# Block-sorted attention and feed-forward: the key products of batches 1 to 3, each split into two matmuls of 64 rows and 64 moving columns

## The chip, the core and the metric

One core of one Trainium2 chip runs one program. The metric is device time in microseconds (us) of one execution: lower is better. The median of three runs of the kernel before is 221.51 us (221.34 to 221.83). One further execution was recorded by the hardware profiler; every number about single instructions comes from that one.

The engines of the core have short names in the profile: PE is the matmul engine, PEld its loads of stationary weights (which run beside PE), DVE the vector engine, ACT the scalar engine, POOL the GpSimd engine, SP the engine whose queue issues DMAs here.

## The reference, cut to what matters

```python
# q, k, v: (4 batches, 8 heads, 768 positions, 64); sort_net: (4, 8, 8, 8)
P = sort_net, normalised five times by exp, rows and columns
k_sorted = einsum('bhij,bhjcd->bhicd', P, k_b)   # 8 blocks of 96 positions, mixed per head
v_sorted = einsum('bhij,bhjcd->bhicd', P, v_b)
scores = softmax(scale * q_b @ k_sorted_b^T)      # block by block, 96 x 96
attn_out = scores @ v_sorted_b                    # x: (3072, 512)
h = maximum(x @ w_in, 0)                          # 512 -> 2048
out = (s * h * h + b) @ w_out                     # 2048 -> 512
```

What matters here is `k_sorted`: for each batch, head and position in a block, the eight blocks' keys are mixed by the head's own 8 x 8 matrix `P`.

## The kernel before, in words

**Layout of the keys.** `RAW["k", b]` holds batch `b`'s keys as 128 partitions by 48 positions by 64 dimensions. A partition is one (head, block, half of the block): 8 heads x 8 blocks x 2 halves, so that partitions 0 to 63 hold heads 0 to 3 and partitions 64 to 127 heads 4 to 7. Mixing the blocks is a matmul that contracts over the partitions. Its moving operand is `PD[b]` (`build_pd`, L273), 128 partitions by `(e, z, g)`: `e` is the parity of the head, `z` the half of the block, `g` the pair of heads times the output block (`NG` = 32). A head's rows meet zeros in every column of another head: of the 128 x 128 numbers, the quarter for rows 0 to 63 and `g` of 16 to 31 is zero, and likewise rows 64 to 127 with `g` of 0 to 15.

**The product that the change touches.** `k_pairs(b, c0, engs)` (L310) makes 16 of the 48 positions. It takes positions two at a time as one stationary operand of 128 columns (2 positions x 64 dimensions), so eight matmuls of 128 rows, 128 stationary and 128 moving columns at L314 fill one PSUM tile `tpp`: two banks, from the pool `psa`, which has three such tiles. Four casts then copy the tile into `KS[b % 2]`, the sorted keys: 64 partitions by 512 numbers each, two on DVE (L205) and two on ACT (L203), through `evac`. `k_pairs` runs three times in a row (`KP(n, 0)`, `KP(n, 1)`, `KP(n, 2)`) for each of batches 1, 2 and 3; batch 0 uses `k_piece` and `k_banks`.

**The order of the work.** Nothing is scheduled automatically: the program's text is the order on each engine, and semaphores wait where data or buffers demand it. The feed-forward works on halves of a batch (`t` = 0 to 7, 384 rows each). `ffn1(t)` (L505) makes eight pieces `hps` at L501 and squares them on ACT (L513) and DVE (L514); `ffn2(t)` (L519) sums 16 matmuls of 512 columns for each of three row blocks at L525 and stores them (`store`, L548). The attention of batch `n` is put between these matmuls by hand: `ffn1` and `ffn2` take `slots`, lists of pieces that are issued after a given step. In `ffn2`, slot 0 comes behind the first four matmuls.

- For batch 1 the three key products stand in slot 3 of `ffn2(0)` and three value products (`v_piece`, L340, tiles `tv`, also from `psa`) in slot 9. The fourth value product and the scores come in `ffn2(1)`.
- For batches 2 and 3 the three key products stand in slot 0 of `ffn2(2b)`. The values take another way: `v_tiles` (L367) in `ffn1(2b)`, then `v_back` (L375), which sends them through DRAM on SP's queue (`vd` at L379, `vs` at L383).
- `s_piece` (L391) makes scores at L405 from `KS` and the transposed queries `qt`: matmuls of 64 rows and 96 moving columns, alternating between rows 0 to 63 and rows 64 to 127, which write different banks of the tile `sc`. `s_banks` (L423) is the same for batch 0. The first two score pieces of batch `n` stand in slot 0 of the `ffn2` that follows the one with the key products. `p_piece` (L433, matmuls at L450) follows in later slots.
- `qt` of batches 1 to 3 comes from `q_dma` (L480), two transposing DMAs on SP's queue (L484) behind `vd` and `vs`. They read `qtok`, which POOL's queue loads (L115) behind the next keys (`rawk`, L93). These loads are held back until the transposed attention output `xt` of the batch before has landed (a one-element POOL copy, L90).

Of the kernel before, what the change touches and what calls it, by code (L numbers as in the profile page):

```python
# [9 lines left out]
FP = mybir.dt.float32  # L10
# [12 lines left out]
def kernel(  # L23
# [12 lines left out]
    nc = tc.nc  # L36
# [14 lines left out]
    NG = NHP * NB  # L51
    VW = D + 2
    CK = 16
# [15 lines left out]
    psa = ctx.enter_context(tc.tile_pool(name="psa", bufs=3, space=bass.MemoryType.PSUM))  # L69
# [14 lines left out]
    RAW = {}  # L84
# [35 lines left out]
    KS = [const.tile([128, NG, 2, GAP], BF, name=f"ks{i}") for i in range(2)]  # L120
# [80 lines left out]
    def evac(eng, out, in_):  # L201
        if eng == "A":
            nc.scalar.copy(out=out, in_=in_)  # L203
        else:
            nc.vector.tensor_copy(out=out, in_=in_)  # L205

    def q_banks(b, half, engs):
# [3 lines left out]
        for u in range(2):  # L211
# [13 lines left out]
            out=jsel, in_=ident.rearrange("p (h j z) -> p j h z", h=H, j=NB), axis=AX.XY, op=ALU.add),  # L225
        lambda: nc.vector.tensor_reduce(
            out=bm.rearrange("p (e z a) -> p e z a", e=2, z=2),
# [26 lines left out]
    PD = {}  # L254
# [54 lines left out]

    def k_pairs(b, c0, engs):  # L310
        m = CK // 2
        ps = psa.tile([128, m, 2, 2 * NG], FP, tag="a", name="tpp")
        for j in range(m):
            nc.tensor.matmul(out=ps[:, j].rearrange("p e g -> p (e g)"),  # L314
                             lhsT=RAW["k", b][:, c0 + 2 * j:c0 + 2 * j + 2, :].rearrange(
                                 "p c d -> p (c d)"),
                             rhs=PD[b].rearrange("p e z g -> p (e z g)"), start=True, stop=True)
        for e in range(2):
            for u in range(2):
                evac(engs[e],  # L320
                     KS[b % 2][e * 64:(e + 1) * 64, :, :, c0 + u:c0 + CK:2],
                     ps[u * 64:(u + 1) * 64, :, e].rearrange("p c (z g) -> p g z c", z=2))

    def k_banks(b, c0, engs):
        for u, eng in enumerate(engs):
# [292 lines left out]
    def KP(b, i, engs="DA"): return lambda: k_pairs(b, i * CK, engs)  # L618
# [93 lines left out]
```

## Time and profile before

| | |
|---|---|
| median of three runs | 221.51 us (221.34 to 221.83) |
| the profiled execution | 221.32 us, span of its instructions 219.6 us |
| granted clock of PE in that execution | 1.0 |
| PE busy | 213.2 us, 97% of the span |
| PEld, DVE, ACT, POOL busy | 128.5, 123.8, 110.8, 71.3 us |
| HBM read and written | 28.85 MB and 7.86 MB |

Busy time is the time in which at least one instruction of the engine was under way. Matmuls are pipelined: one shown with 219 ns can be followed by the next after a quarter of that, so that the spacing of a run of matmuls is its length less one duration, divided by their number less one. In the timeline, a row merges instructions of one kind that follow each other: start, length, engine, line, operation, tiles, shape and count, and in brackets the engine's idle time before it and what ended it. A few matmul records are missing from the trace (L525 has 350 of 368), so counts can be short by one or two.

### The profile page before, as it was taken

The numbers are of one execution on the slowest core, as the hardware profiler recorded it, in microseconds if no ns is written. First come the engines' busy times: TensorE is split into PE (matmuls) and PEld (weight loads), VectorE is DVE, ScalarE is ACT, GpSimd is POOL, SyncE is SP. The second block draws the span as 40 slices with busy tenths as digits, with TensorE's granted clock in tenths as the row PEclk, the third lists the DMA queues.
The fourth block names the chain that finished last, engine by engine and source line by source line (L and its number), as shares of the span: only waits on it lengthen the run. The fifth ranks groups of instructions, "written<-read, shape, count | busy, mean of one in ns | idle before, by whom it ended". The sixth has DMA issues, their size and how long they took to land.

```text
span 219.6 us, 5281 instructions
## 1 busy us (share of the span) xinstructions
PE 213.2 (97%) x2208; PEld 128.5 (59%) x2227; DVE 123.8 (56%) x256; ACT 110.8 (50%) x153; POOL 71.3 (32%) x127
## 2 busy tenths in 40 slices
PE   7999999999999999999999999999999999999994
PEld 5977766655465555556446555666445555654454
DVE  6777456566884767446636686448417744441222
ACT  4687687658626346664622546665425355650000
POOL 7659872689914003950006008720000000000000
DMA  6999999999979753999998955999991580001212
GB/s 155 281 166 124 122 170 207 204 171 139 128 199 136 105 159 62 184 188 117 98 176 198 210 119 74 211 165 95 87 237 51 119 122 0 0 0 51 95 49 96
DMA packets 68023, 28.92 MB, mean 132 GB/s; under 512 B 51872, under 2 KB 64288, under 8 KB 68000
## 3 DMA queue, kind: packets, MB, share of 16 engines
q0 software_dynamic: 31168, 12.85, 50.5%
q1 hardware_dynamic: 36832, 15.74, 39.7%
q8 instruction: 17, 0.28, 0.6%
q14 instruction: 6, 0.05, 0.1%
HBM read 28.85 MB, written 7.86 MB: 167 GB/s over the span
## 4 chain that ended last, share of the span: by engine, by line
PE 96%; DVE 2%; issue 1%; ACT 0%
PE hps L501 38%; PE ops L525 36%; PE z L130 5%; PE pv L450 4%; PE sc L405 3%; PE tpp L314 2%; PE ops L542 2%; PE tv L340 2%; DVE vs L205 1%; PE tr L467 1%; PE scb L423 1%; PE tp L304 1%; PE tvr L367 1%; PE sc L259 0%; PE pv L444 0%
## 5 line engine op out<-in xcount | busy, mean ns | idle before, releaser
L501 PE MATMUL hps<-xt,wi 128*128 128x384 bf16 x512 | 86.6, 326 | 0.0
L525 PE MATMUL ops<-wo,gt 128*128 128x512 bf16 x350 | 82.0, 379 | 1.4 <-issue 0.6
L513 ACT ACTIVATE rt<-hps 128x768 bf16<-128x768 f32 x64 | 51.8, 811 | 37.1 <-PE hps L501 36.4
L501 PEld LDWEIGHTS <-wi 128*128 128x128 bf16 x512 | 48.7, 98 | 32.1 <-issue 0.8
L514 DVE TENSOR_TENSOR gt<-rt 128x768 bf16<-128x768 bf16 x64 | 35.5, 557 | 42.5 <-ACT rt L513 42.4
L525 PEld LDWEIGHTS <-gt 128*128 128x128 bf16 x368 | 34.1, 98 | 37.4
L550 DVE SCALAR_TENSOR_TENSOR ot<-ops,s_bc,bias 128x512 f32<-128x512 f32 (+2 forms) x27 | 18.6, 691 | 34.9 <-PE ops L525 31.1
L413 ACT ACTIVATE at<-sc 112x768 bf16<-112x768 f32 x24 | 18.1, 808 | 30.0 <-PE sc L405 30.0
L456 DVE TENSOR_TENSOR x<-pv,rec 96x512 bf16<-96x512 f32 x32 | 22.0, 686 | 1.1
L115 POOL DMA_DIRECT2D qtok<-in_q_dram x24 | 18.6, 795 | 5.2 <-DMA rawk<-in_k_dram 3.1
L450 PEld LDWEIGHTS <-at 112*128 112x128 bf16 (+1 forms) x256 | 12.8, 101 | 6.7 <-ACT at L413 1.0
L203 ACT CAST ks<-tpp 64x512 bf16<-64x512 f32 x18 | 13.1, 727 | 4.7 <-DVE ks L205 4.1
L140 POOL DMA_DIRECT2D wi<-in_moe_w_in_dram x24 | 13.0, 563 | 4.8 <-DMA rawk<-in_k_dram 3.1
L450 PE MATMUL pv<-vs,at 112*128 112x66 bf16 (+1 forms) x256 | 13.7, 195 | 0.1
L205 DVE CAST ks<-tpp 64x512 bf16<-64x512 f32 x18 | 13.1, 729 | 0.8 <-ACT ks L203 0.5
L93 POOL DMA_DIRECT2D rawk<-in_k_dram x21 | 11.2, 549 | 3.1 <-issue 1.9
L130 PE MATMUL z<-zeros 128*64 128x96 bf16 (+2 forms) x129 | 10.6, 254 | 1.3 <-DVE zeros L118 1.2
L93 POOL DMA_DIRECT2D rawv<-in_v_dram x18 | 9.7, 556 | 5.5 <-DMA wo<-in_moe_w_out_dram 4.0
L90 POOL COPY rawk<-xt 128x1 bf16<-128x1 bf16 x2 | 1.0, 488 | 29.4 <-DMA xt<-x 29.4
L130 PEld LDWEIGHTS <-zeros 128*64 128x64 bf16 (+1 forms) x130 | 8.3, 126 | 3.0 <-DVE zeros L118 1.2
L455 DVE RECIPROCAL rec<-pv 96x8 f32<-96x8 f32 x32 | 6.4, 200 | 6.3 <-PE pv L450 6.3
L90 POOL COPY rawv<-qt 128x1 bf16<-128x1 bf16 x2 | 0.4, 190 | 22.0 <-DMA qt<-qtok 22.0
(98 smaller groups left out, 143.9 us busy)
## 6 DMA issues: line engine op xcount, KB each, us to landing
out_dram<-ot SPq DMA_DIRECT2D x22, 256.0 KB, 2.4
rawv<-in_v_dram POOLq DMA_DIRECT2D x18, 128.0 KB, 5.8
rawk<-in_k_dram POOLq DMA_DIRECT2D x18, 128.0 KB, 4.3
qtok<-in_q_dram POOLq DMA_DIRECT2D x24, 96.0 KB, 7.5
wo<-in_moe_w_out_dram POOLq DMA_DIRECT2D x4, 512.0 KB, 10.4
v0f<-in_v_dram SPq DMA_DIRECT2D x4, 384.0 KB, 5.8
vd<-rawv SPq DMA_DIRECT2D x8, 192.0 KB, 6.3
vs<-vd SPq DMA_DIRECT2D x4, 384.0 KB, 11.9
```

The lines of the kernel that those rows point to most:

```text
L93: nc.gpsimd.dma_start(out=ti[:, c:c + n, :].rearrange("p c d -> p (c d)"), in_=raw["qkv".index(t)][b][:, c * D:(c + n) * D])
L115: nc.gpsimd.dma_start(out=QTOK[b][:, n], in_=qv[:, n])
L130: nc.tensor.matmul(out=z[0:m, 0:w], lhsT=zeros[:, 0:m], rhs=zeros[:, 0:w], start=True, stop=True)
L205: nc.vector.tensor_copy(out=out, in_=in_)
L413: nc.scalar.activation(out=at, in_=sc[0:KR, :, 0:TG], func=AF.Exp, scale=scale)
L450: nc.tensor.matmul(out=pv[0:m, e, n * VW:(n + 1) * VW], lhsT=atf[:, c0:c0 + m], rhs=VS[b % 2][:, e * NG + g(n), :], start=True, stop=True)
L456: nc.vector.tensor_tensor(out=x[:, :, hp * 128:(hp + 1) * 128].rearrange("p n (e d) -> p e n d", e=2), in0=pvv[:, :, :, 0:D], in1=rec.unsq ...
L501: nc.tensor.matmul(out=H1[t, i][:, f, 0:TG], lhsT=wi[:, hp, fc:fc + 128], rhs=XT[t][:, :, hp, :], start=(hp == 0), stop=(hp == NHP - 1))
L513: nc.scalar.activation(out=rt, in_=h, func=AF.Relu)
L514: nc.vector.tensor_tensor(out=gt[:, 2 * i:2 * i + 2, :], in0=rt, in1=rt, op=ALU.mult)
L525: nc.tensor.matmul(out=ops, lhsT=gt[:, f, m * 128:(m + 1) * 128], rhs=wo[:, f, :], start=(f == 0), stop=(f == NF - 1))
L550: nc.vector.scalar_tensor_tensor(out=ot[:, ns], in0=ops, scalar=s_bc, in1=BIAS[0][:, ns], op0=ALU.mult, op1=ALU.add)
```

## The change

Each product of two positions becomes two matmuls: `r` = 0 takes rows 0 to 63 and those 64 moving columns that belong to heads 0 to 3, `r` = 1 takes rows 64 to 127 and the 64 columns of heads 4 to 7. The stationary operand of each has 64 rows and the same 128 columns. The results of `r` = 0 go to the first bank of the tile, those of `r` = 1 to the second. Before, the first four products filled the first bank and the other four the second. The four casts of a tile stay four, on the same engines and in the same order, with 64 partitions by 512 numbers each; their read pattern has one more dimension (`r`), and the step between positions is 64 numbers in place of 128. PE has 72 matmuls and 72 weight loads more. DVE, ACT, POOL and SP issue the same instructions in the same order.

```diff
     def k_pairs(b, c0, engs):
         m = CK // 2
-        ps = psa.tile([128, m, 2, 2 * NG], FP, tag="a", name="tpp")
+        ng = NG // 2
+        ps = psa.tile([128, 2, m, 2, 2, ng], FP, tag="a", name="tpp")
         for j in range(m):
-            nc.tensor.matmul(out=ps[:, j].rearrange("p e g -> p (e g)"),
-                             lhsT=RAW["k", b][:, c0 + 2 * j:c0 + 2 * j + 2, :].rearrange(
-                                 "p c d -> p (c d)"),
-                             rhs=PD[b].rearrange("p e z g -> p (e z g)"), start=True, stop=True)
+            for r in range(2):
+                pr = slice(r * 64, (r + 1) * 64)
+                nc.tensor.matmul(out=ps[:, r, j].rearrange("p e z g -> p (e z) g"),
+                                 lhsT=RAW["k", b][pr, c0 + 2 * j:c0 + 2 * j + 2, :].rearrange(
+                                     "p c d -> p (c d)"),
+                                 rhs=PD[b].rearrange("p e z g -> p (e z) g")[
+                                     pr, :, r * ng:(r + 1) * ng],
+                                 start=True, stop=True)
         for e in range(2):
+            ks = KS[b % 2].rearrange("p (r g) z c -> p r g z c", r=2)[e * 64:(e + 1) * 64]
             for u in range(2):
-                evac(engs[e],
-                     KS[b % 2][e * 64:(e + 1) * 64, :, :, c0 + u:c0 + CK:2],
-                     ps[u * 64:(u + 1) * 64, :, e].rearrange("p c (z g) -> p g z c", z=2))
+                evac(engs[e], ks[:, :, :, :, c0 + u:c0 + CK:2],
+                     ps[u * 64:(u + 1) * 64, :, :, e].rearrange("p r c z g -> p r g z c"))
```

## The prediction

> **What bounds the kernel now.** I read the page's sections 1 and 4 first, then the groups by form, then the timeline around the key products, and at last the landings of the DMAs that the next stage waits for.
>
> ```profile
> PE 213.2 (97%) x2208; PEld 128.5 (59%) x2227; DVE 123.8 (56%) x256; ACT 110.8 (50%) x153; POOL 71.3 (32%) x127
> PE 96%; DVE 2%; issue 1%; ACT 0%
> L314 PE MATMUL tpp<-pd,rawk 128*128 128x128 bf16 x72 | 4.5, 219 | 0.0
> ```
>
> PE is busy without a break and carries 96% of the chain that ended last. Time saved on PE is therefore time saved, as long as PE finds its next data ready. The product in question is 4.5 us of it.
>
> ```profile
> 100.77 0.81 PE L525 MATMUL ops<-wo,gt 128*128 128x512 bf16 x3
> 101.42 1.50 PE L314 MATMUL tpp<-pd,rawk 128*128 128x128 bf16 x24
> 102.76 0.59 PE L525 MATMUL ops<-wo,gt 128*128 128x512 bf16 x2
> ...
> 159.82 1.46 PE L525 MATMUL ops<-wo,gt 128*128 128x512 bf16 x6
> 161.21 0.51 PE L405 MATMUL sc<-qt,ks 64*128 64x96 bf16 x16
> 161.66 1.04 PE L525 MATMUL ops<-wo,gt 128*128 128x512 bf16 x4
> ...
> 60.19 1.71 PE L340 MATMUL tv<-pd,vp 128*64 128x64 bf16 x96
> ```
>
> These are timeline rows of PE: start, length, count. The spacing of a run is (length - one duration) / (count - 1). The 24 key products of batch 2 come (1.50 - 0.219) / 23 = 55.7 ns apart. The scores, whose matmuls alternate between the two halves of the rows, come (0.51 - 0.203) / 15 = 20.5 ns apart, 41 ns for a pair of 96 columns. The values, which alternate between two halves of the columns and move 64, come (1.71 - 0.197) / 95 = 15.9 ns apart, 32 ns for a pair. So two half-array matmuls run side by side, and a pair costs about what one stream costs.
>
> ```profile
> 102.37 8.76 SPq L484 DMA_TRANSPOSE qt<-qtok  x1
> DMA to landing us min/median/max: 10.7/10.7/10.7
> ...
> 113.23 0.52 PE L405 MATMUL sc<-qt,ks 64*128 64x96 bf16 x16
> DMA to landing us min/median/max: 9.0/9.0/9.0
> ```
>
> The first query transpose of batch 2 is issued at 102.37 and lands 10.7 us later, at 113.1. The first scores of batch 2, which read it, start at 113.23. That is no slack at all. The same transpose of batch 3 (second landing line, issued at 151.11) lands at 160.1, 1.1 us ahead of its scores at 161.21. Batch 1's landed at 60.4, scores at 65.15.
>
> **The stage, added up.** *Before*, from the start of the last L525 matmul ahead of it to the first one behind it: the products begin 101.42 - (100.77 + 0.81 - 0.379) = 0.22 us after that matmul, run 23 x 0.0557 = 1.28, and the next L525 starts 0.06 after the last of them (102.76 - 102.70). Sum 1.56 us.
>
> *After*: the array goes from whole to halves and back. The scores show what that costs: they begin 161.21 - (159.82 + 1.46 - 0.379) = 0.31 us after the last L525 matmul, and the next starts 161.66 - (161.21 + 0.51 - 0.203) = 0.14 after the last score. That is 0.09 + 0.08 = 0.17 us more than now. Between lie 48 matmuls, 47 spacings. No row has 64 rows by 128 columns with 64 moving columns. The scores bound it from above: same stationary form, half as many columns again, 20.5 ns. The values bound it from below: same 64 moving columns, stationary of 128 x 64, 15.9 ns. I take the values' row, because the spacing should follow the moving columns: 96 against 64 is 1.5, and 20.5 against 15.9 is 1.3. The weight loads are no bound: the first two pairs of loads of a score piece stand 15 ns apart. Then 0.31 + 47 x 0.0159 + 0.14 = 1.20 us, a gain of 0.36 us per batch. By the scores' row it is 0.31 + 0.96 + 0.14 = 1.41, a gain of 0.15. The break-even spacing is (1.56 - 0.45) / 47 = 23.6 ns.
>
> The moving operand now comes in four runs of 16 numbers. The scores of batch 0 (L423) read runs of 16 as well and keep the same spacing, so I count nothing. The two matmuls of a pair write different banks, as the scores do.
>
> **A rule against it.** The Trainium skill's page "TensorE: Matmul & The Clock Gate", section "Back-to-back issue gap", gives 1 to 64 moving columns a floor of about 60 cycles, some 25 ns, and "TensorEngine Tiling (Array Packing)", section "Instruction Overhead", warns against taking a tiling factor from a dimension that is already small. By that floor for each matmul the stage would be 0.31 + 47 x 0.025 + 0.14 = 1.63 us, no gain. This trace disagrees: the values' 64-column matmuls come every 15.9 ns, 96 in a row.
>
> **The casts.** DVE and ACT copy 64 x 512 numbers as before, with one dimension more.
>
> ```profile
> L205 DVE CAST ks<-tpp 64x512 bf16<-64x512 f32 x18 | 13.1, 729 | 0.8 <-ACT ks L203 0.5
> 55.72 4.50 DVE L205 CAST ks<-tpp 64x512 bf16<-64x512 f32 x6 [0.45 <-ACT ks L203]
> ```
>
> I count them at nothing, since the number of elements is the same and the step was long before, too. Bounds: no saving, and at worst a doubling. In batches 2 and 3 they end about 5 us before the scores. In batch 1 they are cover: the third value product (64 matmuls after 60.19, at 61.2; 60.85 with the gain) needs the last key tile, whose casts on DVE end at 60.22. As ACT starts a little earlier (the first tile is full about 0.08 us sooner), this becomes 60.14. Slack 0.7 us over eight casts in a chain (two on ACT, six on DVE): they may grow from 0.73 to 0.82 us before PE waits. In batches 2 and 3 the third key tile needs the buffer of the last `hps`, read by ACT until 101.57 in batch 2; its products move from 102.31 to 102.02, still behind it.
>
> **What becomes of the gain.** Batch 1: nothing waits, 0.36 us passes on. The loads and transposes of batch 2 hang on `xt` of batch 1, which hangs on PE, so they come 0.36 earlier with it. Batch 2: the chain of loads, `vd`, `vs` and `qt` starts at 84 to 86 us, before this batch's key products at 101.4. It doesn't gain from them, so PE only arrives 0.36 us too early at the scores and waits for `qt`. Gain 0. Batch 3: slack 1.1 us, 0.36 passes on. Nothing later waits for a DMA (`xt` lands some 4 us before its use), and PE sets the end. Sum: 0.36 + 0 + 0.36 = 0.72. On the profiled 221.32 us that is 220.60. The median of the runs is 0.19 above the profiled execution; carried along, this gives **220.8**.
>
> **Rivals.**
> *All three batches pass.* POOL's first key load for batch 2 started 1.74 us after its predecessor, for nothing the profile shows:
>
> ```profile
> 86.64 1.08 POOL L93 DMA_DIRECT2D rawk<-in_k_dram  x2 [1.74 <-issue]
> 133.18 1.06 POOL L93 DMA_DIRECT2D rawk<-in_k_dram  x2 [0.30 <-POOL rawk L90]
> ```
>
> In batch 3 it was 0.30. If the 1.4 us are chance, `qt` usually lands about a microsecond earlier, and batch 2 gains as well: 3 x 0.36 = 1.08, 220.4. Against it: the program on POOL is the same, and so may the pause be.
> *The spacing of the scores.* 0.15 for each of two batches, 0.30: 221.2, three batches 221.1. For it: the same stationary form. Against: 64 columns less 96.
> *Single file, slower.* If the two matmuls of a product don't overlap, they cost what 66 columns cost in one file, as in the eight L450 matmuls that start at 167.06 and take 0.42 us: (0.42 - 0.207) / 7 = 30 ns each. 0.31 + 47 x 0.030 + 0.14 = 1.86, 0.30 us more per batch, 0.9 in all: 222.4. It decides above 23.6 ns. Against it stand the scores, which have the same two halves of rows and overlap.
> *Casts that double, slower.* From 0.82 us on, batch 1 pays: at 1.22 us (DVE's cast of twice the elements, `vs<-tv`) the chain of eight is 3.9 us longer, less 0.7 of slack, so 3.2 us of waiting, less 0.36 in batch 3: 224.4. For it: one more dimension. Against: one element after another is read in either form.
> *A floor for each small matmul.* If a matmul costs something of its own however few its columns, the spacing ends between the values' 15.9 and the single file's 30 ns; at the break-even of 23.6 nothing is gained, 221.5. By the Trainium skill's 25 ns (the section named above) the estimate is three times 0.07 us more, 221.7. The chance is small, by the values' row.
>
> **How the numbers follow.** Two runs of this kernel differ by about 0.2%, so less can't be told from no change; that is 0.44 us. Chances: forecast 0.45, all three batches 0.22, spacing of the scores 0.11, single file 0.07, casts 0.06, floor 0.03, and 0.06 for what I don't see, mostly slower. Forecast and all three are faster by over 0.2%: 0.67, and a part of the scores' case, 0.02, with it. Within 0.2%: the rest of the scores' case, a part of the floor and of the unseen: 0.14. Slower: 0.17. The range runs from 220.1 (all three, less the 0.19 between profile and median, and a little) to 221.6, past the scores' case; the slower cases, 0.17, are left out.
>
> **What would show it.** Right: each stage of 48 `tpp` matmuls about 0.75 + 0.2 us long in the timeline; the L525 matmul behind it 1.2 us after the one ahead; casts of 0.73 us; in batch 2, scores that start within 0.2 us of the landing of `qt`, with PE idle ahead of them; in batch 3, scores with slack left. Wrong: spacings above 20 ns, casts above 0.82 us and PE waiting for DVE at L340, or batch 2's scores starting without a wait (then 220.4).

## The result, and the profile after

| | before | changed |
|---|---|---|
| median of 22 runs each | 221.73 us | 220.76 us |
| ratio of the runs, 95% interval | | 0.9957 (0.9944 to 0.9971) |
| the profiled execution | 221.32 us, span 219.6 | 221.41 us, span 219.6 |

The change saves 0.43%, about 0.95 us (0.64 to 1.24). The profiled execution of the changed kernel is one of its slowest, as slow as before. That makes it a useful one: it shows the gain and three places that take it back.

First the page and the groups by form of the changed kernel. Its lines L317, L345, L410, L506 and L530 are L314, L340, L405, L501 and L525 of the kernel before.

```profile
PE 212.1 (97%) x2280; PEld 126.8 (58%) x2299; DVE 123.7 (56%) x256; ACT 110.9 (50%) x153; POOL 71.0 (32%) x127
PE 82%; DMA 9%; SPq 4%; DVE 3%; issue 1%; ACT 1%
L317 PE MATMUL tpp<-pd,rawk 64*128 64x64 bf16 x144 | 2.6, 190 | 0.0
L205 DVE CAST ks<-tpp 64x512 bf16<-64x512 f32 x18 | 13.1, 728 | 0.3
```

The products, twice as many, keep PE busy for 2.6 us in place of 4.5. The casts are as long as before (728 ns, 729 then). The chain that ended last now leads through DMAs for 13% of the span, where it was PE for 96%: in this execution PE waited for data.

The timeline of PE around batch 2's products (start, length, engine, line, count, idle time before):

```profile
100.65 0.81 PE L530 MATMUL ops<-wo,gt 128*128 128x512 bf16 x3
101.39 0.87 PE L317 MATMUL tpp<-pd,rawk 64*128 64x64 bf16 x48
102.42 10.31 PE L530 MATMUL ops<-wo,gt 128*128 128x512 bf16 x47 [0.16 <-issue]
113.51 0.52 PE L410 MATMUL sc<-qt,ks 64*128 64x96 bf16 x16 [0.78 <-DMA qt<-qtok]
```

The stage begins 0.31 us after the last L530 matmul (100.65 + 0.81 - 0.379 = 101.08), its 47 spacings take 0.87 - 0.190 = 0.68 us, 14.6 ns each, and the next L530 starts 0.135 us behind (the row at 102.42 lacks its first record, one spacing of 0.216; the sums over whole parts in the last table below bear this out). Sum 1.13 us, against 1.56 before: **0.43 us gained in each batch**. All three stages of every run with these products agree to 0.001 us. In the trace the two matmuls of a pair start 3 to 4 ns apart and the next pair follows some 26 ns later, so that each half takes one matmul every 29.3 ns and both do so at once.

Then PE stands idle for 0.78 us ahead of the scores, until `qt` has landed: batch 2's gain is gone, and as much again. The transpose was issued 0.5 us earlier than before and took 11.5 us to land, 10.7 before; it landed at 113.4, PE was there 0.85 us sooner than it could start. The pause of POOL ahead of the key loads, which I had thought might be chance, is there again:

```profile
101.83 9.19 SPq L489 DMA_TRANSPOSE qt<-qtok  x1
DMA to landing us min/median/max: 11.5/11.5/11.5
...
86.51 1.08 POOL L93 DMA_DIRECT2D rawk<-in_k_dram  x2 [1.74 <-issue]
```

It was 1.73 to 1.76 us long in all 14 executions that were profiled in this study. In batch 3 the scores don't wait, as forecast; they begin 0.31 us behind the last L530 matmul (two records are missing around the rows at 150.83 and 161.74):

```profile
149.79 0.87 PE L317 MATMUL tpp<-pd,rawk 64*128 64x64 bf16 x48
150.83 10.31 PE L530 MATMUL ops<-wo,gt 128*128 128x512 bf16 x47 [0.16 <-issue]
161.07 0.51 PE L410 MATMUL sc<-qt,ks 64*128 64x96 bf16 x16
```

The two smaller losses are at the value products of batch 1 and ahead of the first L506 behind batch 3:

```profile
55.65 0.75 DVE L555 SCALAR_TENSOR_TENSOR ot<-ops,s_bc,bias 128x512 f32<-128x512 f32 x1 [1.81 <-POOL bias L617]
56.43 4.50 DVE L205 CAST ks<-tpp 64x512 bf16<-64x512 f32 x6
59.87 1.90 PE L345 MATMUL tv<-pd,vp 128*64 128x64 bf16 x96
```

The 96 value products take 1.90 us in place of 1.71, with one gap of 0.197 us at 61.07, where the third needs the last key tile; its casts end at 60.93. They ended at 60.22 before. The casts take no longer than before; they began later, because DVE's addition of the bias ahead of them waited until 55.65 for POOL (54.52 before).

The transposing DMA that makes the first `xt` of batch 3, with the instruction queue in its time (packets, MB, share) where it has a packet, and the first matmuls that read this `xt`, before and then after:

```profile
xt<-x SPq DMA_TRANSPOSE x1, 3.9
174.89 0.82 PE L501 MATMUL hps<-xt,wi 128*128 128x384 bf16 x4
```

```profile
q8 instruction: 1, 0.02, 1.0%
xt<-x SPq DMA_TRANSPOSE x1, 5.4
174.96 0.83 PE L506 MATMUL hps<-xt,wi 128*128 128x384 bf16 x4
```

It takes 5.4 us to land, not 3.9: it lands at 174.92 in place of 173.50, and L506 starts 0.22 us late. A packet of instructions (queue q8, 16 KB) falls into its time.

From the L525 matmul ahead of batch 1's products to the last output matmul, the two profiled executions take 163.08 and 163.05 us. 3 x 0.43 = 1.28 gained, 0.19 + 0.85 + 0.22 given back. How often the three waits come, and how much, is the question of the experiments.

### The profile page after: what moved, and what is told of

It is laid out like the page before. It is cut to its first block, busy times and chain, and to the rows that moved or that the text cites. A ratio compares the mean times of both kernels' runs of the same rounds, so it can differ in the third digit from the quotient of the medians.

```text
span 219.6 us, 5425 instructions
## 1 busy us (share of the span) xinstructions
PE 212.1 (97%) x2280; PEld 126.8 (58%) x2299; DVE 123.7 (56%) x256; ACT 110.9 (50%) x153; POOL 71.0 (32%) x127
## 4 chain that ended last, share of the span: by engine, by line
PE 82%; DMA 9%; SPq 4%; DVE 3%; issue 1%; ACT 1%
PE ops L530 31%; PE hps L506 31%; DMA qt<-qtok 5%; PE z L130 5%; PE pv L455 4%; DMA vd<-rawv 3%; SPq L388 3%; PE sc L410 3%; PE tv L345 2%; PE ops L547 2%; DVE vs L205 1%; SPq L384 1%; PE tpp L317 1%; PE tr L472 1%; PE scb L428 1%
## 5 line engine op out<-in xcount | busy, mean ns | idle before, releaser
L506 PE MATMUL hps<-xt,wi 128*128 128x384 bf16 x512 | 86.6, 326 | 0.1
L530 PE MATMUL ops<-wo,gt 128*128 128x512 bf16 x350 | 81.5, 379 | 1.7 <-issue 1.1
L506 PEld LDWEIGHTS <-wi 128*128 128x128 bf16 x512 | 48.7, 98 | 32.3 <-issue 0.8
L530 PEld LDWEIGHTS <-gt 128*128 128x128 bf16 x368 | 34.0, 98 | 37.6
L130 PE MATMUL z<-zeros 128*64 128x96 bf16 (+2 forms) x129 | 10.7, 255 | 1.3 <-DVE zeros L118 1.2
```

Source lines behind the costliest of these rows:

```text
L130: nc.tensor.matmul(out=z[0:m, 0:w], lhsT=zeros[:, 0:m], rhs=zeros[:, 0:w], start=True, stop=True)
L506: nc.tensor.matmul(out=H1[t, i][:, f, 0:TG], lhsT=wi[:, hp, fc:fc + 128], rhs=XT[t][:, :, hp, :], start=(hp == 0), stop=(hp == NHP - 1))
L530: nc.tensor.matmul(out=ops, lhsT=gt[:, f, m * 128:(m + 1) * 128], rhs=wo[:, f, :], start=(f == 0), stop=(f == NF - 1))
```

## The experiments

Ratios are to the kernel before, run on the same chip, with 95% intervals.

**One batch at a time.** `k_pairs` takes the split products for one batch and the whole ones for the others:

```diff
     def k_pairs(b, c0, engs):
+        if b != 1:                      # 2 in only2, 3 in only3
+            return k_whole(b, c0, engs) # k_pairs of the kernel before
```

> Only batch 1 has the split products. In the profile of the changed kernel a stage of key products went from 1.56 to 1.13 us between the L525 matmuls around it (entry 0.31, 48 matmuls in 0.68, exit 0.135), so a batch gains 0.43 us at its place. Theory (batch 2's gain is lost at the wait for its query transpose, the others pass on): 0.25 to 0.43 us faster than before, the loss being a wait of the third value product for the casts on DVE, 0.15 us in that profile. Rival (all three pass alike, and the gain is 0.95 / 3): 0.32 us. This run alone does not tell them apart; with the next two it does.

> Only batch 2 has the split products. Theory: the chain of loads that ends in batch 2's query transpose starts ahead of these products and is not moved by them, so PE comes 0.43 us too early to the first scores and waits: no change within 0.2 us, and idle time of PE ahead of the first scores (near 113 us) that ends with the landing of qt. Rival (the pause of POOL ahead of the key loads is chance, qt is usually early): 0.3 to 0.43 us faster, no idle time there.

> Only batch 3 has the split products. Both theories: 0.43 us faster, since the query transpose of batch 3 had landed about 1 us ahead of its use before. If it is less than 0.2, slack of batch 3 was chance and something else takes the gain.

Measured: 0.9994 (0.9973 to 1.0015), 0.9987 (0.9966 to 1.0008) and 0.9990 (0.9967 to 1.0013). Single runs scatter over 1 to 2 us, so the times tell none of the three apart from nothing. The traces do (L333, L361, L426, L522 and L546 are these five lines there, and L314 the old products). In only1 the values lose 0.22 us, the first L522 behind batch 1 waits 0.12 us for `xt`, and the scores of batch 2 wait, although that batch's products are the old ones:

```profile
101.45 1.50 PE L314 MATMUL tpp<-pd,rawk 128*128 128x128 bf16 x24
102.79 10.52 PE L546 MATMUL ops<-wo,gt 128*128 128x512 bf16 x47
113.74 0.52 PE L426 MATMUL sc<-qt,ks 64*128 64x96 bf16 x16 [0.42 <-DMA qt<-qtok]
```

So `qt` doesn't land at a fixed distance behind PE's own work; here it came at 113.60. In only3 it came at 112.91, and the scores didn't wait; they start 0.31 us behind the last L546 matmul (103.04 + 10.52 - 0.379 = 113.18):

```profile
101.70 1.50 PE L314 MATMUL tpp<-pd,rawk 128*128 128x128 bf16 x24
103.04 10.52 PE L546 MATMUL ops<-wo,gt 128*128 128x512 bf16 x47
113.49 0.51 PE L426 MATMUL sc<-qt,ks 64*128 64x96 bf16 x16
```

That run gains its full 0.43 us behind batch 3's products (66.81 us to the end, 67.24 before). The profiled execution of only2 was held up by 2.5 us ahead of batch 2's products, 1.9 of them at the first L522 behind batch 1, whose `xt` landed 7.25 us after its issue, so that it can't say whether batch 2 waits by itself.

**Is it two halves side by side, or fewer columns?** Two kernels keep every size and count. One exchanges the two loops, the other lets both matmuls use the same half:

```diff
-        for j in range(m):
-            for r in range(2):
+        for r in range(2):              # single_file
+            for j in range(m):
```
```diff
-                pr = slice(r * 64, (r + 1) * 64)
+                pr = slice(0, 64)       # one_half
```

> The split products of all three batches with the two loops exchanged: first the eight matmuls of rows 0 to 63, then the eight of rows 64 to 127, so that neighbours use the same half of the array. Theory (the gain comes from two halves that stream side by side): spacing near 30 ns as in the pv matmuls, stage 0.31 + 47 x 0.030 + 0.135 = 1.86 us, 0.30 us longer than before in each batch, 0.9 us slower than before in all (222.4). Rival (the gain comes from half as many moving columns, whatever the order): spacing near 15 ns and the time of the changed kernel, 0.95 us faster than before.

> The changed kernel, but both matmuls of a product take rows 0 to 63 of keys and of PD (the keys of heads 4 to 7 are left out: that part of the result is zero). Number, sizes and order of all instructions are the same; only the other half of the array never takes part. Theory (the gain is two halves side by side): about 29 ns from one matmul to the next, as in the first matmuls of single_file; stage 0.31 + 47 x 0.029 + 0.135 = 1.81 us, 0.25 us per batch longer than before, 0.5 to 0.8 us slower than before. Rival (it is the smaller number of columns, and loads that are quicker with 64 rows): spacing 15 ns, as the changed kernel.

Measured: single_file 0.9970 (0.9954 to 0.9986), faster; one_half 1.0037 (1.0015 to 1.0060), slower by 0.8 us. The products of batch 2, single_file first:

```profile
101.72 1.08 PE L317 MATMUL tpp<-pd,rawk 64*128 64x64 bf16 x48
```

```profile
101.80 1.57 PE L317 MATMUL tpp<-pd,rawk 64*128 64x64 bf16 x48
```

With one half the spacing is (1.57 - 0.19) / 47 = 29.4 ns, the stage 1.82 us, 0.27 longer than before. Three times 0.27 is the 0.8 us. So 64 columns in one file cost 29 ns, twice 14.6: the gain is two halves at once. What sets the 29 ns of one half, the columns or the weight loads, which come just as far apart, no run shows. The miss is single_file: I had expected 1.86 us there and it takes 1.33, a gain of 0.22 a batch; 3 x 0.22 is the 0.66 us measured. Its first five matmuls stand 29 to 40 ns apart, then most spacings fall to 8 to 21. The order of the program is not the order of the starts; more on that at the end.

**Room at the three waits.** In after_late the first two score pieces of batch 2 come one slot later; before_late is the kernel before with that move. after_slack also moves the values, after_q1 instead reads the queries of batch 1, and after_room and before_room add a move for `xt`:

```diff
+        if n == 2:                      # late, slack, room
+            s1[1] = s1.pop(0) + s1[1]
-                  9: [V(n, 0, "D"), V(n, 1, "A"), V(n, 2, "D")]}
+                  10: [V(n, 0, "D"), V(n, 1, "A"), V(n, 2, "D")]}  # slack, room
+        if n == 3:                      # room
+            s1 = {i - (3 <= i <= 6): p for i, p in s1.items()}
```
```diff
+        qb = 1 if b == 2 else b         # after_q1, in s_piece
-                    r = QT[b][pr, half * HB + n, hp, :]
+                    r = QT[qb][pr, half * HB + n, hp, :]
```

> The changed kernel, with the first two score pieces of batch 2 one slot later (behind eight L525 matmuls of that pass in place of four), 0.86 us later on PE. Theory (in the changed kernel batch 2's gain is lost, in whole or in part, at the wait for the query transpose): no idle time of PE ahead of these scores, and all three gains of 0.43 us pass: 1.1 to 1.3 us faster than before, 0.2 to 0.4 faster than the changed kernel. Rival (the wait is rare): the time of the changed kernel, 0.95 us faster than before.

> The kernel before with the same move of the first two score pieces of batch 2. Theory: the transpose lands at about the time at which PE comes to the scores, so that before has at most a short wait to lose: 0 to 0.3 us faster. If it is faster by 0.5 us or more, before already stood at that wait in most runs. If it is slower, the move itself costs something, and the comparison has to allow for it.

> The run after_late, and the three value products of batch 1 one slot later too (behind the eleventh group of four L525 matmuls in place of the tenth). Theory: the third of them no longer waits for the casts of the last key tile on DVE (0.15 us in the profile of the changed kernel): 1.2 to 1.3 us faster than before, spacing of all value products even. Rival: that wait is made up elsewhere, and the time is that of after_late.

> The changed kernel, but all scores of batch 2 are computed from the transposed queries of batch 1, which landed some 50 us earlier; the transposes of batch 2 still run. So these scores wait for no transpose at any place. Theory: as after_late, 1.1 to 1.3 us faster than before, no idle time of PE near 113 us. Rival: 0.95 us as the changed kernel.

> The run after_slack, and in the last pass of scores (batch 3) the four pieces behind slots 3 to 6 one slot earlier, so that the transposed output xt has 0.86 us more to land before the next L501 matmuls. Three waits take part of the gain in single executions: the third value product of batch 1 for the casts (0.15 to 0.2 us), the scores of batch 2 for qt (0 to 0.8), the first L501 behind batch 3 for xt (0.03 to 0.22). Here each has room. Theory (these waits, and nothing else, stand between 3 x 0.43 and the measured 0.95): 1.28 us faster than before, and in the trace no gap of PE behind 53 us above 0.1 us but the changes from whole to half array. Rival (the gain is eaten by something that these waits do not show): 0.95 us as the changed kernel.

> The kernel before with the same three moves. Theory: before has these waits rarely or for less, so the moves alone bring 0 to 0.2 us, and after_room stays about 1.28 us ahead of this run. Rival: the moves alone bring 0.3 us or more; then they, and not the split products, make after_room faster than the changed kernel.

> The changed kernel once more, on the same chip as the other three. Both theories: 0.6 to 1.2 us faster than before. Its trace tells how large the three waits named for after_room are in another execution: up to 0.2 us at the value products, 0 to 0.8 us at the scores of batch 2, up to 0.2 us at the first L501 behind batch 3.

| run | ratio, 95% interval | us less than before |
|---|---|---|
| after_late | 0.9961 (0.9944 to 0.9977) | 0.86 |
| before_late | 0.9999 (0.9988 to 1.0011) | 0.02 |
| after_slack | 0.9960 (0.9946 to 0.9975) | 0.89 |
| after_q1 | 0.9963 (0.9944 to 0.9983) | 0.82 |
| again | 0.9955 (0.9930 to 0.9979) | 1.00 |
| after_room | 0.9942 (0.9921 to 0.9963) | 1.28 |
| before_room | 0.9995 (0.9961 to 1.0029) | 0.11 |

The row of after_slack rests on 6 runs, the others on 12. Taking the wait for `qt` away brings nothing that these times can show: 0.86 and 0.82, where 1.1 to 1.3 was expected. Their intervals reach to 1.24 us, so the times alone don't rule that theory out; the traces below show the wait in some executions and not in others. after_slack, expected at 1.2 to 1.3, has 0.89, though its value products come without a gap. Room at all three places gives 1.28 us, the sum of the three gains, and the moves alone give 0.11. But the interval of after_room runs from 0.46 to 1.75 us and overlaps that of the changed kernel, so that it is the best of the runs, not shown to be better than the change alone. Nor did its trace come out as expected: there was a wait at a place where I had left no room, the first L506 behind batch 1, 0.37 us later than usual:

```profile
78.87 0.99 PE L506 MATMUL hps<-xt,wi 128*128 128x384 bf16 x5 [0.21 <-DMA xt<-x]
```

This fourth wait is no work of the split alone: in before_late, whose products are all old, the same place lost 0.29 us.

The traces tell more than the times. PE time in us from the L525 matmul ahead of one batch's products to that ahead of the next batch's, and from batch 3's to the last output matmul ("changed" is the execution shown above):

| profiled execution | 1 to 2 | 2 to 3 | 3 to end | sum | where gain was lost |
|---|---|---|---|---|---|
| before | 47.85 | 48.00 | 67.24 | 163.08 | |
| before_room | 47.84 | 47.98 | 67.24 | 163.06 | |
| one_half | 48.11 | 48.24 | 67.58 | 163.94 | xt 0.06 |
| changed | 47.61 | 48.40 | 67.04 | 163.05 | values 0.19, qt 0.85, xt 0.22 |
| again | 47.45 | 47.55 | 67.05 | 162.04 | xt 0.02 and 0.23 |
| after_room | 47.80 | 47.55 | 66.81 | 162.16 | xt 0.37 |

47.42, 47.55 and 66.81 are what each part of the changed kernel comes to without a wait; each is 0.43 to 0.45 us less than before. In the run again, the same program as the changed kernel, batch 2 loses nothing:

```profile
100.94 0.87 PE L317 MATMUL tpp<-pd,rawk 64*128 64x64 bf16 x48
101.98 10.31 PE L530 MATMUL ops<-wo,gt 128*128 128x512 bf16 x47 [0.16 <-issue]
112.22 0.51 PE L410 MATMUL sc<-qt,ks 64*128 64x96 bf16 x16
```

`qt` landed at 111.92 there, ahead of PE. Over the twelve profiled executions other than only2 and one_half it landed between 111.2 and 113.6. Of the six with all three batches split in pairs, PE would have had to wait for it in three (0.4 to 0.85 us; in two of them the moved or replaced scores hid that) and not in the other three.

## Why the prediction was right, and where it was not

The time was right, 220.8 forecast and 220.76 measured, and so was the sign. That the two are so close is luck: the forecast took 0.72 us off the median of three runs, 221.51, and the medians of 22 runs are 221.73 and 220.76, 0.97 us apart. A gain 0.25 too small and a start 0.22 too low cancel. Of its steps:

- *The stage.* Entry 0.31 and exit 0.14 came as taken from the scores (0.31 and 0.135). The mechanism, two halves side by side, was right. The spacing was mis-sized: 15.9 ns by the values' row, 14.6 measured, so 0.68 us in place of 0.75 and a gain of 0.43 in place of 0.36. The bounds were wrong too: the values were no lower bound.
- *The casts* were rightly counted at nothing (728 ns). The slack of 0.7 us at the third value product was read from one execution; it depends on when POOL delivers the bias. In the changed kernel's profile it was used up, 0.19 us.
- *What becomes of the gain* is the step that failed. "Gain 0" for batch 2 took one execution's landing for a property of the kernel. The rival in which all three pass is no better as a rule, and its condition was wrong: POOL's pause is no chance, it is in every execution. `qt` lands early in one execution and late in the next all the same. The mechanism is there (0.78 us of idle time that ends with `qt`), but PE would have met it in only three of the six profiled executions with all three batches split in pairs, too few to say how often it comes.
- *"Nothing later waits for a DMA (`xt` lands some 4 us before its use)"* was a misreading: 4 us is the time from issue to landing. In the profile of before the first `xt` of batch 3 lands at 173.50 and is used at 174.89, 1.4 us of slack; those of batches 1 and 2 have 0.7 us (landed at 78.22 and 126.18, used at 78.92 and 126.91). In all the executions with three split stages that left it no room, batch 3's slack was used up, and up to 0.23 us were lost there.
- The forecast 0.72 against the measured 0.95 is thus made of terms that partly cancel: 0.14 too little by the spacing of the two batches that were to pass; for batch 2, 0.43 too little where `qt` is early, and as much too much where it is as late as in the changed kernel's profile (0.85 lost against 0.43 gained); and 0.04 to 0.42 too much by waits at the values and for `xt`, in the six executions. The median comes near for that reason too.
- *The rivals.* The scores' spacing and single file are refuted by the 14.6 ns, casts that double by their 728 ns; one_half shows the price of a single file, 0.8 us slower (0.9 forecast). The floor of some 25 ns in the Trainium skill's "TensorE: Matmul & The Clock Gate", section "Back-to-back issue gap", does not hold for two halves together (14.6 ns). Within one half the trace of one_half has 29.4 ns, above it.

That the whole of the difference between 1.28 and 0.95 comes from these waits is likely, since the sums of the traces close to 0.03 us, but it is not shown: how the waits are spread over the runs without a trace stays open, and the kernel before waits in some executions too.

## What to carry to other kernels

A product in which each half of the rows meets only zeros in half of the columns can be split into two half-array matmuls that stream side by side. Here that nearly halved the time from the first product to the last (1.28 to 0.68 us) and cost 0.17 us for going to halves and back, so put many such products in a row. Before a gain on the busiest engine is counted, list every transfer that lands within that gain ahead of its use, and take the spread of its landing over several executions, since one trace gives one draw. Added instructions can move transfers, too: with the 72 more matmuls the packets of the instruction queue came at other times.

## What the runs showed of the hardware

**Halves overtake each other.** In single_file 42 of the 47 spacings are between neighbours of the same half. At the 29.4 ns of one_half they alone would take 1.23 us; the whole run took 0.89. And by the trace the 17th matmul of the program, the first of the second tile, which waits on ACT's semaphore, is the 14th to start. So a matmul of one half starts ahead of earlier ones that still queue for the other half. The Trainium skill's page "TensorE: Matmul & The Clock Gate", section "The mechanism", says that matmuls start in program order; these starts disagree. Nor does it hold for the starts of such halves that the program's text is the order on each engine, as was said ahead of the prediction.

**One transposing DMA landed later where a packet of the instruction queue fell into its time.** Over 14 profiled executions, the first `xt` of batch 3 landed 5.2 to 5.4 us after its issue in the eight whose PE program has all 144 matmuls, and 3.84 to 3.87 in the six others. In each of the eight a 16 KB packet of the instruction queue begins 2.8 to 3.4 us after the issue, in none of the six. Before, the nearest packets were at 168.3 and 177.7 us; the second fell into the next `xt`, which took 4.6 us in place of 3.8. No run moved the packet alone, so this is a correlation, without an exception at this place. Elsewhere there are exceptions: in after_q1 the first `xt` of batch 2 took 5.1 us with no such packet, and in only3 the second `qt` of batch 1 took 3.8 us with one that began 3.2 us after its issue.
